# Inputs and outputs in the kernel's own shapes: q turned, k and v stacked, weights tiled before the launch

## The chip, the cores and the metric

One core of a Trainium2 chip. The metric is the device time of one execution in microseconds, the median of the runs. Engines: TensorE (PE: matmul; PEld: its weight load), VectorE (DVE), ScalarE (ACT), GpSimd (POOL), and SyncE (SP), whose queue issues nearly all DMAs. TensorE's clock has two levels, 1.2 and 2.4 GHz; the profile gives the granted share of the upper one.

## The reference

`q`, `k`, `v` are 8 batches x 8 heads x 576 tokens x 64, in float32; `w_in` (512 x 2048) and `w_out` (2048 x 512) are handed over in float64.

```python
kv  = einsum('bhsd,bhse->bhde', k, v)          # 64 x 64 per head
out = einsum('bhsd,bhde->bhse', q, kv)
x   = out / sqrt(mean(out**2, -1) + 1e-6) * g_norm   # per token and head
x   = x.transpose(0, 2, 1, 3).reshape(4608, 512)
h   = x @ w_in
y   = (h * cos(h)) @ w_out                     # 4608 x 512, float32
```

## The kernel before

**Chunks and stages.** The 4608 tokens are cut into 9 chunks of 512. A chunk lies across one or two of the 8 blocks (batches) of 576. In each chunk the features of x are four pairs of heads, p = 0 to 3, a tile of 128 features x 512 tokens each. Every large product runs in three parts, as a float32 number is split into a high and a low half that TensorE takes at full rate: high x high, low x high, high x low. Chunks 0 to 2 are plain: for each of the 16 tiles j of `w_in` and `w_out` a step computes h (12 products of 512 columns) and adds to four accumulators (12 more). The steps' order is in `segments` (line 315): chunk 0 with j 0 to 3, chunk 1 with j 0 to 7, chunk 0 with j 4 to 15, chunk 1 with j 8 to 15, chunk 2. Step 4 is so the first of chunk 1. Chunks 3 to 8 go in pairs with seven products in place of eight; of the last pair, 7 and 8, the second product is made so too, with its output turned (features x tokens).

**Front and steady state.** Blocks 0 and 1 and chunks 0 and 1 have a path of their own (`kv_front_part`, `x_front_part`) in full float32: k'v is accumulated over 9 or 6 slices of tokens, q arrives with tokens in partitions, is turned by TensorE in four transposes, copied by ScalarE or VectorE into a `two` tile, and multiplied; then come the norm (ScalarE square, VectorE reduce, GpSimd power, VectorE multiply), another turn by TensorE, and the split into xhi and xlo. For the later blocks `kv_part` makes k'v: 512 tokens of a head in four slices and a fifth slice with the leftover 64 tokens, padded with zeros to 128 rows in `k_over`, `v_over`. `x_part` turns q with VectorE (32x32 blocks; the DMA brings it in pieces of 32 values). Chunks 2 to 4 (`THREE`) then take three products, with k'v as blocks on a diagonal; chunks 5 to 8 take two, with high and low halves packed beside each other, into two PSUM banks whose halves ScalarE and VectorE add. `kv_turn_part` repacks k'v between the two forms.

**Weights.** `w_part` makes float32 out of the float64 words: ScalarE reads the high word, ScalarE or VectorE the low word, two operations of VectorE join them, then ScalarE rounds to the high half and VectorE subtracts. The split tiles are also stored to DRAM and reloaded by the later chunks (`wq`, `wod`, `wos`), partly as sums (`sums_part`, `sums_out_part`).

**What sets the order.** The program is written by a planner (`Order`, line 50): generators ask for an engine and a duration, and at each point the work item with the earliest start goes next, on a tie that with the smallest priority. A priority is a due time plus an entry of the table `haste` (line 343, `put_off`); `step_off` shifts gates by a quarter of the entry. Where two engines are offered (`copiers`, `adders`, the low word), the planner takes the one that it expects to end first. The order is fixed in the program (`Pinned`), for SP's DMAs too. Tokens (`t_two` with five, `t_slot`, `t_bank`) stand for buffers. SP keeps at most eight transfers under way: each issue waits for the landing of the eighth before it.

**The end.** The last products leave turned; `leave` and `finale` turn them back with VectorE in 32x32 blocks and store them in pieces of 32 values, four DMAs a tile.

Nearly all instructions carry line 253, the wrapper that pins the order, so the profile is read by tile names and shapes.

Of the kernel before, what the change touches and what calls it, by code (L numbers as in the profile page):

```python
# [9 lines left out]
F32 = mybir.dt.float32  # L10
# [8 lines left out]

P = 128  # L20
# [5 lines left out]


# [171 lines left out]
def tile_kernel(  # L199
# [3 lines left out]
    k: bass.AP,  # L203
    v: bass.AP,
    g_norm: bass.AP,
    moe_w_in: bass.AP,
    moe_w_out: bass.AP,
# [3 lines left out]
    B, H, S, D = q.shape  # L211
    NT, DM = out.shape
    DFF = moe_w_in.shape[1]
    NP = H // 2
    NJ = DFF // P
    CH = 512
    NCH = NT // CH
# [5 lines left out]
    assert ST == D  # L223
# [4 lines left out]
    SF = 2 * S // P  # L228
    SP = 96
    SQ = S // SP  # L230
# [76 lines left out]
    k_over = const.tile([P, H, D], F32, name="k_over")  # L307
    v_over = const.tile([P, H, D], F32, name="v_over")
    for t in (k_over, v_over):
        pool.memset(t, 0.0)  # L310
# [21 lines left out]
    THREE = (2, 3, 4)  # L332
    ASIDE = (3, 4)

    def due(i):
# [7 lines left out]
    haste = {  # L343
        ('acc', 0): -22.3, ('acc', 1): -60.4, ('acc', 10): -24.7, ('acc', 11): 82.8, ('acc', 12): -40.9,
        ('acc', 13): 546.1, ('acc', 14): 62.7, ('acc', 15): -8.6, ('acc', 16): 1346.9, ('acc', 17): 182.9,
        ('acc', 19): 223.9, ('acc', 2): 245.4, ('acc', 20): 41.4, ('acc', 21): 469.9, ('acc', 22): -280.7,
        ('acc', 23): 10.3, ('acc', 24): -146.3, ('acc', 25): 53.8, ('acc', 26): 1836.1, ('acc', 27): 138.4,
        ('acc', 28): -1.3, ('acc', 29): -8.2, ('acc', 3): 7.7, ('acc', 30): 74.1, ('acc', 31): -138.7,
        ('acc', 32): 0.1, ('acc', 33): -261.8, ('acc', 34): -11.5, ('acc', 35): 2337.3, ('acc', 36): -151.0,
        ('acc', 37): -973.0, ('acc', 38): 134.4, ('acc', 39): 5.1, ('acc', 4): 833.1, ('acc', 40): 39.8,  # L350
        ('acc', 41): 6.6, ('acc', 42): -789.5, ('acc', 43): 21.8, ('acc', 44): -19.0, ('acc', 45): 71.8,
        ('acc', 46): -3.6, ('acc', 47): -203.1, ('acc', 5): 233.3, ('acc', 6): 171.0, ('acc', 7): -97.9,
        ('acc', 8): 605.9, ('acc', 9): -64.2, ('act', 0): -4.7, ('act', 1): -343.2, ('act', 10): -435.4,
        ('act', 11): -15.0, ('act', 12): 49.5, ('act', 13): 1.5, ('act', 14): 142.2, ('act', 15): 354.9,
        ('act', 17): 152.2, ('act', 18): 110.4, ('act', 19): -139.7, ('act', 2): 0.9, ('act', 20): -58.3,
        ('act', 21): -47.2, ('act', 22): -435.2, ('act', 23): 1.8, ('act', 24): 43.9, ('act', 25): 7.6,
        ('act', 26): 47.9, ('act', 27): 4.6, ('act', 28): 50.6, ('act', 29): 236.4, ('act', 3): 37.6,
        ('act', 30): 4.8, ('act', 31): 55.4, ('act', 32): -148.1, ('act', 33): 146.1, ('act', 34): -1.6,
        ('act', 35): 10.6, ('act', 37): 48.3, ('act', 38): -3.0, ('act', 39): -35.2, ('act', 4): -93.7,
        ('act', 40): -126.6, ('act', 41): 254.3, ('act', 42): -133.3, ('act', 43): 71.5, ('act', 45): 112.7,  # L360
        ('act', 46): 148.3, ('act', 47): 530.0, ('act', 6): -5.1, ('act', 7): -6.8, ('act', 8): 26.3,
        ('act', 9): -250.2, ('combine by', 0, 0, 0): -12.5, ('combine by', 0, 0, 1): 479.5,
# [12 lines left out]
        ('cross', 0, 1): -12.2, ('cross', 1, 0): 327.2, ('cross', 1, 1): 659.3, ('cross', 2, 0): 132.8,  # L375
        ('cross', 2, 1): -59.2, ('fin', 0, 0): 199.4, ('fin', 0, 1): 34.5, ('fin', 0, 3): 782.3,
        ('fin', 0, 4): 21.1, ('fin', 0, 6): -37.3, ('fin', 0, 7): -143.6, ('fin', 1, 0): -26.5, ('fin', 1, 1): -3.5,
        ('fin', 1, 2): 126.4, ('fin', 1, 3): -24.4, ('fin', 1, 5): 171.4, ('fin', 1, 7): -2.8, ('fin', 2, 1): 15.2,
        ('fin', 2, 2): 2.6, ('fin', 2, 3): 437.1, ('fin', 2, 4): -402.0, ('fin', 2, 5): -194.2,
        ('fin', 2, 6): -186.8, ('fin', 2, 7): 227.9, ('fin', 3, 1): -283.5, ('fin', 3, 2): 1.6, ('fin', 3, 3): 27.7,  # L380
        ('fin', 3, 4): -31.5, ('fin', 3, 5): 196.1, ('fin', 3, 6): 214.6, ('fin', 3, 7): 166.8, ('fin', 4, 0): 53.6,
        ('fin', 4, 1): 16.5, ('fin', 4, 2): -114.1, ('fin', 4, 3): 203.6, ('fin', 4, 4): 39.6, ('fin', 4, 5): 134.7,
        ('fin', 4, 6): -188.8, ('fin', 4, 7): 10.3, ('fin', 5, 0): -127.7, ('fin', 5, 1): 146.9,
        ('fin', 5, 3): -81.5, ('fin', 5, 4): 98.9, ('fin', 5, 5): 100.8, ('fin', 5, 6): 25.0, ('fin', 5, 7): 109.9,
        ('fin', 6, 0): -147.6, ('fin', 6, 1): -13.5, ('fin', 6, 2): -21.2, ('fin', 6, 3): -25.8,
        ('fin', 6, 4): -193.3, ('fin', 6, 5): -30.4, ('fin', 6, 6): 438.9, ('fin', 6, 7): 408.9,
# [157 lines left out]
    def chunk_parts(c):  # L544
        parts, t = [], c * CH
        while t < (c + 1) * CH:
# [3 lines left out]
            t = e  # L550
        return parts

    def front_rows(c):

        if c == 0:
            return [(0, 0, P, 0), (0, 0, P, 1)]
# [1458 lines left out]
```

## Time and profile before

| | |
|---|---|
| runs | 822.45, 822.56, 823.3 us; median 822.56 |
| profiled execution, span | 823.5 us; no other time of it is given |
| TensorE busy | 808.5 us (98%), 4319 matmul instructions |
| VectorE, ScalarE, GpSimd busy | 658.0 (80%), 519.6 (63%), 315.7 us (38%) |
| DMA | 195.90 MB, 238 GB/s; 92080 of 183794 packets under 512 B |
| granted clock | 0.998 of full speed |

Busy times count each engine's instructions; an engine may be busy and yet wait for nothing that matters. In the trace a tile name stands for a buffer that serves several purposes: `wi` and `wo` hold weights, but in front also k, v, q and k'v; `m` and `sg` are the two halves of a `two` tile; `bank` and `acc` are PSUM. In a matmul row `128*64 128x64` means 128 rows and 64 columns of the array in use and a result of 128 x 64 places; a full float32 product is several instructions. Matmul records overlap, so what one costs is read from the distance of starts.

### The profile page before, as it was taken

What the parts mean: (1) busy time and instruction counts of PE and PEld (TensorE: products, weight loads), DVE (VectorE), ACT (ScalarE), POOL (GpSimd) and SP (SyncE); (2) the same over time, 40 slices, a digit from 0 to 9 for tenths busy, and PEclk for the clock granted to TensorE, in tenths of its full rate; (3) what the DMA queues carried; (4) which work ended last, traced back from release to release, by engine and by line L of the source; (5) the groups of instructions that cost most, each with busy time, mean ns of one, the idle gap of its engine ahead of it and who ended that gap; (6) DMA issues with size and microseconds to landing.
All of it is one profiled execution on the core that took longest, in us unless ns stands there. A gap on an engine that the chain in (4) does not pass through costs nothing.

```text
span 823.5 us, 12898 instructions
## 1 busy us (share of the span) xinstructions
PE 808.5 (98%) x4319; PEld 668.4 (81%) x4319; DVE 658.0 (80%) x1032; ACT 519.6 (63%) x1014; POOL 315.7 (38%) x212
## 2 busy tenths in 40 slices
PE   8889999999999999999999999999999999999997
PEld 7668888888888888887888888888888888888886
DVE  4989999568588897899997368889788888787862
ACT  5857897446545556787885646786586666675440
POOL 3234203136253352234567702224544402353450
PEclk9999999999999999999999999999999999999999
DMA  9997535667656858797797777897887788757763
GB/s 292 341 337 283 197 120 180 219 168 257 153 130 208 288 171 281 241 280 271 215 305 242 260 259 240 259 335 228 277 238 247 257 281 305 254 183 255 212 191 58
DMA packets 183794, 195.90 MB, mean 238 GB/s; under 512 B 92080, under 2 KB 145840, under 8 KB 183728
## 3 DMA queue, kind: packets, MB, share of 16 engines
q1 hardware_dynamic: 182672, 194.95, 75.4%
q8 instruction: 34, 0.56, 0.3%
q14 instruction: 32, 0.26, 0.1%
q10 hardware_dynamic: 1056, 0.13, 0.1%
HBM read 149.95 MB, written 45.09 MB: 237 GB/s over the span
## 4 chain that ended last, share of the span: by engine, by line
PE 91%; DMA 5%; DVE 2%; ACT 1%; SPq 0%; issue 0%; POOL 0%; ACTq 0%; POOLq 0%; DVEq 0%
PE bank L253 51%; PE acc L253 39%; DMA wo<-in_moe_w_out_dram 2%; DMA wi<-in_moe_w_in_dram 1%; DMA wi<-in_v_dram 1%; DMA wo<-wq 1%; DMA wi<-in_q_dram 1%; DVE sg L253 1%; SPq L253 0%; DVE r L253 0%; DVE glo L253 0%; ACT slot L253 0%; ACT sg L253 0%; POOL sg L253 0%; ACT wi L253 0%
## 5 line engine op out<-in xcount | busy, mean ns | idle before, releaser
L253 PE MATMUL bank<-wi,wo 128*128 128x512 f32 (+2 forms) x1284 | 287.7, 379 | 2.2 <-DMA wi<-in_v_dram 1.6
L253 PE MATMUL acc<-wo,ghi 128*128 128x512 f32 x896 | 277.1, 390 | 0.0
L253 PEld LDWEIGHTS bank<-wi,wo 128*128 128x128 f32 (+2 forms) x1284 | 227.0, 184 | 50.6 <-issue 2.4
L253 PEld LDWEIGHTS acc<-wo,ghi 128*128 128x128 f32 x896 | 167.1, 188 | 34.3
L253 PE MATMUL acc<-wo,glo 128*128 128x512 f32 x448 | 174.6, 390 | 0.0
L253 POOL TENSOR_TENSOR rinv<-ms,mhalf 128x16 f32<-128x16 f32 (+1 forms) x36 | 98.9, 2757 | 130.5 <-DVE ms L253 130.2
L253 PE MATMUL bank<-xhi,wi 128*128 128x512 f32 x320 | 99.6, 392 | 0.1
L253 PEld LDWEIGHTS acc<-wo,glo 128*128 128x128 f32 x448 | 84.1, 188 | 17.7
L253 DVE TENSOR_TENSOR wi<-bank,wi 128x512 f32<-128x512 f32 x72 | 49.2, 686 | 28.7 <-PE bank L253 23.8
L253 PEld LDWEIGHTS bank<-xhi,wi 128*128 128x128 f32 x320 | 59.5, 188 | 12.8 <-ACT wo L253 0.5
L253 ACT ACTIVATE ki<-wi 128x512 int32<-128x512 f32 x72 | 45.2, 628 | 28.6 <-DVE wi L253 24.7
L253 PE MATMUL bank<-xlo,wi 128*128 128x512 f32 x160 | 62.4, 390 | 0.0
L253 ACT COPY wi<-bank 128x512 f32<-128x512 f32 x72 | 42.0, 585 | 22.3 <-PE bank L253 21.2
L253 ACT ACTIVATE ki<-bank 128x512 int32<-128x512 f32 x72 | 42.7, 593 | 19.7 <-PE bank L253 15.2
L253 ACT ACTIVATE r<-r 128x512 f32<-128x512 f32 x60 | 37.8, 629 | 22.1 <-DVE r L253 20.9
L253 ACT CAST ghi<-r 128x512 fp32r<-128x512 f32 x57 | 35.3, 620 | 25.5 <-PE acc L253 24.6
L253 DVE TENSOR_TENSOR glo<-r,ghi 128x512 fp32r<-128x512 f32 x51 | 39.3, 773 | 13.8 <-ACT ghi L253 13.5
L253 ACT ACTIVATE wo<-wo 128x512 f32<-128x512 f32 x59 | 37.0, 629 | 15.7 <-DVE wo L253 15.0
L253 ACT CAST ghi<-wo 128x512 fp32r<-128x512 f32 x44 | 27.3, 619 | 23.7 <-PE acc L253 22.7
L253 DVE TENSOR_TENSOR r<-r,bank 128x512 f32<-128x512 f32 x50 | 33.9, 679 | 4.7 <-ACT r L253 3.8
L253 DVE SCALAR_TENSOR_TENSOR r<-bank,ki 128x512 f32<-128x512 f32 x51 | 34.7, 681 | 2.8 <-ACT ki L253 2.4
L253 POOL TENSOR_TENSOR glo<-wo,ghi 128x512 fp32r<-128x512 f32 x18 | 24.3, 1348 | 31.6 <-ACT ghi L253 30.3
(230 smaller groups left out, 1325.0 us busy)
## 6 DMA issues: line engine op xcount, KB each, us to landing
wo<-wq SPq DMA_DIRECT2D x84, 512.0 KB, 4.7
wo<-wod SPq DMA_DIRECT2D x64, 512.0 KB, 5.0
wi<-in_moe_w_in_dram SPq DMA_DIRECT2D x16, 512.0 KB, 10.1
wo<-in_moe_w_out_dram SPq DMA_DIRECT2D x16, 512.0 KB, 10.0
wod<-wo SPq DMA_DIRECT2D x16, 512.0 KB, 4.0
wo<-wos SPq DMA_DIRECT2D x16, 512.0 KB, 3.6
out_dram<-slot SPq DMA_DIRECT2D x28, 256.0 KB, 4.3
wq<-wi SPq DMA_DIRECT2D x24, 256.0 KB, 3.6
```

The source lines that it names most:

```text
L253: return lambda *a, **kw: tc.keep_in_program_order(f(*a, **kw))
```

## The change

`kernel()` now prepares the arrays: q transposed to features x tokens per chunk and pair; k and v stacked per block and pair into tiles of 128 partitions, of which each holds eight slices of 64 values and, behind them, the leftover tokens of head 0 in partitions 0 to 63 and of head 1 in 64 to 127; g_norm twice; weights tile by tile with 4 KB per partition. The kernel writes its output tile by tile, and `kernel()` transposes those of chunks 7 and 8 and joins them. Removed are the turns of q (TensorE in front, VectorE later) and of the last outputs, `k_over`, `v_over`, the packed two-product form with `kv_turn_part`. In front, k'v runs over the same five slices as later, kv_front has one block-diagonal tile per pair instead of two padded ones, and the x product of chunk 1 takes five pieces per pair instead of ten. `sums_out_part` gets a wait. The table of priorities is replaced as a whole (`HASTE`, not shown but for the entries of the first loads).

```diff
-def tile_kernel(ctx, tc, q, k, v, g_norm, moe_w_in, moe_w_out, out)
+def tile_kernel(ctx, tc, q, kv, g_norm, wi_words, wo_words, out)
...
+    ('load kv', 0, 0): -10.9, ('load kv', 0, 2): 102.7, ('load kv', 1, 0): -1.9, ('load kv', 1, 3): -1.6,
+    ('load q', 0, 2): -15.0, ('load q', 0, 3): -6.3, ('load q', 1, 1): -14.3, ('load q', 1, 3): 194.8,
...
     def kv_loads(b, p):
-            kv_tiles[b, p] = [two(slot, [P, 2, SI, D], F32, n) for n in range(2)], slot
-            for t, src in zip(kv_tiles[b, p][0], (k, v)):
-                sync.dma_start(
-                    out=t, in_=src[b, 2 * p:2 * p + 2, 0:SI * P, :].rearrange("h (p i) d -> p h i d", i=SI))
+            kv_tiles[b, p] = [two(slot, [P, KV], F32, n) for n in range(2)], slot
+            for n, t in enumerate(kv_tiles[b, p][0]):
+                sync.dma_start(out=t, in_=kv[b, p, n])
...
     def q_loads(c, p):
-            for b, s0, o0, n in chunk_parts(c):
-                for j in range(2):
-                    for f in range(2):
-                        ...
-                        sync.dma_start(out=qb[...], in_=q[...].rearrange("(tb t) d -> t tb d", t=32))
+            t = at.tile([P, CH], F32, name=f"qb{slot}", bufs=1)
+            sync.dma_start(out=t, in_=q[c, p])
...
+    def kv_products(ps, kt, vt):
+        def parts(i, j):
+            if i < SI:
+                cols = slice((SI * j + i) * D, (SI * j + i + 1) * D)
+                return kt[:, cols], vt[:, cols]
+            return kt[rows_of[j], KV - D:KV], vt[rows_of[j], KV - D:KV]
+        for i in range(SI + 1):
+            for j, r in enumerate(rows_of):
+                lhs, rhs = parts(i, j)
+                pe.matmul(out=ps[r, :], lhsT=lhs, rhs=rhs, start=(i == 0), stop=(i == SI))
...
     def x_front_part(c, p, prio):
         yield "wait", [q_in[c, p]]
-        pair = yield "take", t_two, prio
-        ...
-        for n in range(NTT):
-            pe.transpose(out=ps_t[:, n * P:(n + 1) * P], in_=qn[:, n, :], identity=ident)
-        e, end = yield "run", copiers(), prio
-        qT = two(pair, [P, CH], F32, 0)
-        copy(e, qT, ps_t[:, 0:CH])
...
+        qT = q_tiles.pop((c, p))
+        for b, _, o0, n in parts:
+            t = o0
+            while t < o0 + n:
+                e = min(t - t % P + P, o0 + n)
+                pe.matmul(
+                    out=ps[t % P:t % P + e - t, t - t % P:t - t % P + P], lhsT=qT[:, t:e],
+                    rhs=kv_front[b][:, p, :], start=True, stop=True)
+                t = e
...
     def x_part(c, p, prio):
-        dve.transpose(out=qT, in_=qb.rearrange("p a b -> p (a b)"))
-        if c in THREE:
-            yield from x_blocks(c, p, prio, parts, qT, slot)
-            return
-        ... (two products into two banks, halves joined)
+        qT, q_slot = q_tiles.pop((c, p))
         qhi, qlo = (two(slot, [P, CH], F32R, j) for j in range(2))
-        e, end = yield "run", copiers(), prio
-        copy(e, qhi, qT)
+        e, end = yield "run", [("ACT", act_us(), 0.0), ("DVE*", dve_us(), 0.3)], prio
+        copy(e.rstrip("*"), qhi, qT)
...
     def sums_out_part(m, prio):
+        yield "wait", [wo_kept[2 * m], wo_kept[2 * m + 1]]
         yield "take", t_sums, prio
...
         def finale(bank, v):
-            dve.transpose(out=o, in_=bank)
-            store(LAST, 1, v, o, slice(0, CH), [sync, act, sync, act])
+            act.copy(out=o[:, 0:half], in_=bank[:, 0:half])
+            act.dma_start(out=out[LAST, 2 + v, :, 0:half], in_=o[:, 0:half])
+            dve.tensor_copy(out=o[:, half:CH], in_=bank[:, half:CH])
+            sync.dma_start(out=out[LAST, 2 + v, :, half:CH], in_=o[:, half:CH])
...
 def kernel(**inputs):
+    arrays["q"] = q.transpose(1, 3, 0, 2).reshape(NP, P, NCH, CH).transpose(2, 0, 1, 3)
+    kv = _np.stack([x.reshape(B, NP, 2, S, D) for x in (k, v)], 2)
+    main = kv[:, :, :, :, :SI * P].reshape(B, NP, 2, 2, P, SI, D).transpose(0, 1, 2, 4, 3, 5, 6)
+    over = kv[:, :, :, :, SI * P:].reshape(B, NP, 2, P, D)
+    arrays["kv"] = _np.concatenate([main.reshape(B, NP, 2, P, 2 * SI * D), over], -1)
...
+    tiles = [x.reshape(CH, CH) for x in got]
+    return _np.concatenate([x.T if c in TURNED else x for c, x in enumerate(tiles)], 0)
```

## Rows read from the trace of the kernel before

**Rows 1.** Chain of waits from 60 us: start, duration, what.

```profile
64.84 9.55 PE bank L253 x42
...
136.95 16.32 PE bank L253 x72
```

**Rows 2.** Busy us (count) per engine by stretch; granted clock, DMA share, GB/s.

```profile
0.00:26.57 26.57, 21.54 (x316) 18.54 (x316) 14.85 (x32) 15.96 (x38) 11.35 (x17) 1.00 0.99 294
26.57:63.70 37.13, 32.63 (x232) 24.18 (x230) 33.07 (x57) 25.37 (x53) 11.62 (x7) 1.00 1.07 348
63.70:818.55 754.85, 754.28 (x3777) 625.68 (x3775) 609.31 (x944) 478.25 (x924) 292.78 (x189) 1.00 0.74 232
```

**Rows 3.** Chain of waits up to 70 us.

```profile
7.89 7.96 DMA wi<-in_v_dram
```

**Rows 4.** DMA issues up to 32.6 us: count, KB each, us to landing.

```profile
wi<-in_moe_w_in_dram SPq DMA_DIRECT2D x8, 512.0 KB, 9.6
wo<-in_moe_w_out_dram SPq DMA_DIRECT2D x5, 512.0 KB, 10.2
```

**Rows 5.** Timeline of VectorE: start, duration, what, idle time before it.

```profile
45.09 0.43 DVE L253 TENSOR_SCALAR m<-wo 128x512 int32<-128x512 uint32 x1 [2.56 <-DMA wo<-in_moe_w_out_dram]
```

**Rows 6.** Timeline of SP's issues.

```profile
39.44 5.34 SPq L253 DMA_DIRECT2D wo<-in_q_dram  x3
```

**Rows 7.** Groups of instructions up to 64 us: busy us, mean ns, idle before.

```profile
L253 ACT COPY m<-bank 128x512 f32<-128x512 f32 x8 | 4.5, 586 | 1.7 <-PE bank L253 1.7
...
L253 DVE TENSOR_SCALAR m<-wi 128x512 int32<-128x512 uint32 x4 | 1.7, 422 | 0.0
...
L253 DVE COPY wo<-bank 64x64 f32<-64x64 f32 x6 | 1.3, 224 | 6.8 <-ACT wo L253 5.1 <-PE bank L253 1.7
...
L253 DVE TENSOR_SCALAR m<-wo 128x512 int32<-128x512 uint32 x3 | 1.3, 424 | 2.6 <-DMA wo<-in_moe_w_out_dram 2.6
```

**Rows 8.** Timeline of TensorE around four q products, first and next piece.

```profile
169.42 0.34 PE L253 MATMUL bank<-m,kv_w 128*128 128x128 f32 x2
...
170.29 0.40 PE L253 MATMUL acc<-wo,ghi 128*128 128x512 f32 x1
...
215.20 0.37 PE L253 MATMUL bank<-m,kv_w 128*128 128x192 f32 x2
...
215.97 0.62 PE L253 MATMUL bank<-xhi,wi 128*128 128x512 f32 x2
...
365.58 0.41 PE L253 MATMUL bank<-m,kv_w 128*128 128x320 f32 x2
...
366.08 0.41 PE L253 MATMUL acc<-wo,ghi 128*128 128x512 f32 x1
...
411.68 0.41 PE L253 MATMUL bank<-m,kv_w 128*128 128x384 f32 x2
...
412.21 0.68 PE L253 MATMUL acc<-wo,ghi 128*128 128x512 f32 x2
```

**Rows 9.** Timeline of TensorE, begin of a k'v product.

```profile
161.04 0.39 PE L253 MATMUL acc<-wo,glo 128*128 128x512 f32 x1
161.36 0.69 PE L253 MATMUL bank<-sg,m 128*64 128x64 f32 x16
161.88 0.29 PE L253 MATMUL bank<-v_over,k_over 128*64 128x64 f32 x4
161.99 0.64 PE L253 MATMUL bank<-sg,m 128*64 128x64 f32 x16
```

**Rows 10.** Timeline of the end, all engines.

```profile
818.59 0.72 DVE L253 STREAM_TRANSPOSE slot<-bank 128x512 f32<-128x512 f32 x1 [4.72 <-PE bank L253]
...
819.34 0.93 ACTq L253 DMA_DIRECT2D out_dram<-slot  x2
```

**Rows 11.** Busy us by stretches of 20 us.

```profile
120.00:140.00 20.00, 20.00 (x90) 16.55 (x89) 20.00 (x32) 17.50 (x32) 3.04 (x3) 1.00 0.55 155
140.00:160.00 20.00, 20.00 (x90) 16.57 (x89) 12.32 (x18) 8.74 (x16) 6.18 (x5) 1.00 0.81 270
```

More of the change, by code (lines that the diff above doesn't have):

```diff
@@ L538, in put_off @@
+    haste = HASTE
     def put_off(*key):
@@ L608, in g_part @@
         yield "wait", [kv_in[0, 1]]
-        _, end = yield "run", [("ACT", 0.4)], -11.0
-        for r in (slice(D, 2 * D), slice(0, D)):
-            act.activation(out=gcol[r, :], in_=gcol[0:D, :], func=AF.Copy, scale=INV_2PI)
+        _, end = yield "run", [("ACT", 0.2)], -11.0
+        act.activation(out=gcol, in_=gcol, func=AF.Copy, scale=INV_2PI)
         sched.fire(g_both, end)
@@ L727, in kv_front_part @@
         bank = yield "take", t_bank, prio
-        _, end = yield "run", [("PE", 0.7 if b else 1.05)], prio, D if b else 0
+        _, end = yield "run", [("PE", 0.65)], prio, D
         ps = ps_tile(bank)
         kt, vt = kv_tiles.pop((b, p))
-        heads = [slice(j * D, (j + 1) * D) for j in range(2)]
-        n = SQ if b else SF
-        for i in range(n):
-            for j, r in enumerate(heads):
-                lhs, rhs = (t[0:SP, j, i, :] if b else t[r, i, :] for t in (kt, vt))
-                pe.matmul(out=ps[r, 0:D], lhsT=lhs, rhs=rhs, start=(i == 0), stop=(i == n - 1))
+        kv_products(ps[:, 0:D], kt, vt)
         sched.fire(kv_used[b, p], end)
@@ L740, in copies @@
         def copies(j):
-            e, end = yield "run", [("ACT", 0.41, 0.0), ("DVE", 0.45, 0.3)], prio
-            for r in heads:
-                copy(e, kv_front[b][r, 2 * p + j, r], ps[heads[j], 0:D])
+            e, end = yield "run", [("ACT", 0.2, 0.0), ("DVE", 0.22, 0.1)], prio
+            r = rows_of[j]
+            copy(e, kv_front[b][r, p, r], ps[r, 0:D])
             sched.fire(done[j], end)
@@ L832, in kv_split_part @@
         yield "wait", [kv_done[b, p] for p in range(NP)]
-        front = kv_front[b].rearrange("p (n j) d -> p n j d", j=2)
-        rows = [slice(j * D, (j + 1) * D) for j in range(2)]
-        end = yield from kv_parts(b, [front[r, :, j, r] for j, r in enumerate(rows)], prio)
+        end = yield from kv_parts(b, [kv_front[b][r, :, r] for r in rows_of], prio)
         for p in range(NP):
@@ L939, in x_part @@
         sched.fire(x_took[c, p], 0.0)
-        yield "take", t_qT
-        _, end = yield "run", [("DVE", dve_us())], prio
-        qT = at.tile([P, CH], F32, name="qT", bufs=1)
-        qb, q_slot = q_tiles.pop((c, p))
-        dve.transpose(out=qT, in_=qb.rearrange("p a b -> p (a b)"))
-        sched.give(t_q, end, q_slot)
-        rows = [slice(j * D, (j + 1) * D) for j in range(2)]
-        if c in THREE:
-            yield from x_blocks(c, p, prio, parts, qT, slot)
-            return
-        qs = [two(slot, [P, CH], F32R, j) for j in range(2)]
@@ L951, in x_part @@
-        for j, r in enumerate(rows):
-            yield "run", [("ACT", act_us())], prio
-            act.copy(out=qs[j][r], in_=qT[r])
-            e, end = yield "run", adders(CH, put_off("x by", c, p)), prio
-            adder(e).tensor_tensor(out=qs[j][rows[1 - j]], in0=qT[r], in1=qs[j][r].bitcast(F32), op=ALU.subtract)
-        sched.give(t_qT, end)
-        yield "wait", [(kv_turned if b in turned else kv_done)[b, p] for b, _, _, _ in parts]
-        yield "take", t_pair, prio
-        banks = []
@@ L960, in x_part @@
-        for j in range(2):
-            yield "take", t_psa, prio
-            banks.append((yield "take", t_bank, prio))
-        _, end = yield "run", [("PE", sum(2 * max(0.11, (n + 32) / 2400) for _, _, _, n in parts))], -1.0
-        both = [ps_tile(bank) for bank in banks]
-        for j in range(2):
-            for b, s0, o0, n in parts:
-                pe.matmul(
-                    out=both[j][:, o0:o0 + n], lhsT=kv_w[:, b % 2, 2 * p + j, :], rhs=qs[j][:, o0:o0 + n],
-                    start=True, stop=True)
@@ L970, in x_part @@
-        sched.fire(q_used[c, p], end)
-        sched.give(t_two, end, slot)
-        x, held = yield from x_place(c, prio)
-        for j, r in enumerate(rows):
-            ps = both[j]
-            yield "run", [("ACT", act_us())], prio
-            act.copy(out=x[r], in_=ps[rows[1 - j], 0:CH])
-            _, end = yield "run", [("DVE", dve_us())], prio
-            dve.tensor_tensor(out=x[r], in0=ps[r, 0:CH], in1=x[r], op=ALU.add)
-            give_ps(banks[j], end)
-        sched.give(t_pair, end)
@@ L1259, in out_part @@
         if complete:
-            sync.dma_start(out=rows(c, t), in_=o)
+            sync.dma_start(out=out[c, t], in_=o)
         else:
@@ L1851, in part_done @@
             elif v == 0:
[L1852 removed]
+                sched.spawn(leave(LAST, 1, 0, bank, 0.5), t)
             else:
```

436 lines of the change are left out of this document (154 added, 282 removed), and 177 rows, old and new, of tables (HASTE, haste).

## Prediction, before the result was known

> **What bounds the kernel now.** I read the chain of waits first: from 64.84 us on its long pieces are matmuls [rows 1]. Next the busy times by stretch [rows 2]: from 63.70 to 818.55 us TensorE has 0.57 us of idle time in 754.85 at the full granted clock, so in there only TensorE's own work counts, and what another engine saves is worth nothing while it stays ahead. Before 63.70 it is different: only the four first steps of chunk 0 have run, 4 x 24 products of 512 columns, 21.8 us at the 0.227 us that one takes in a full stretch (16.32 us for 72 [rows 1]). The rest of these 63.70 us is the front: loads, attention products of chunks 0 and 1, weight splitting. There VectorE is the busiest engine after TensorE (33.07 of 37.13 us [rows 2]) and DMA is full (share 0.99 and 1.07). After the last matmul stands a tail of 823.5 - 818.55 = 4.9 us. So the time is: when step 4 (the first of chunk 1) starts, at 64.84 [rows 1]; plus the TensorE work from there; plus the tail. I price the change in these three.
>
> **The start of step 4.** Four terms.
> (a) Block 0's loads. The last of them was issued at 7.89 and landed at 15.85 [rows 3]. Up to there came block 0 (8 x 288 KB of k and v, 4 x 256 KB of q: 3.41 MB) and one 0.52 MB tile of w_in, 3.93 MB in all. The new priorities (base times plus HASTE) put every load of block 0 ahead of w_in. At the stretch's 294 GB/s [rows 2] the 0.52 MB are 1.8 us. The x product of a pair then no longer waits for four TensorE transposes and a copy out of PSUM (0.59 us each [rows 7]). I take 3.0 us: 1.8, two such copies in a row, nothing for the transposes. Bounds: 1.8 and 5.
> (b) The wait for weights. VectorE stood 2.56 us until 45.09 for a tile of w_out [rows 5]. Until 32.6 us eight tiles of w_in had been issued but five of w_out [rows 4], and the second half of chunk 1's q (512 KB) was issued only from 39.44 us [rows 6]. Steps 0 to 3 need four of each. By the new priorities all of block 1 and these eight tiles come before the fifth pair: 3.41 + 3.41 + 8 x 0.524 = 11.0 MB, at 294 to 348 GB/s 32 to 37 us, against 45 and more now. The wait goes: 2.6 us. Next in line is VectorE itself, not another load. Bounds: 1 and 2.6.
> (c) VectorE's own work in front. Splitting a weight tile has one operation, the low word, that the planner gives to ScalarE or VectorE; VectorE did seven of these at 0.42 us. ScalarE now loses 8 copies of 0.586 us (4.5 us busy [rows 7]) and half of its 64x64 copies, so it can take them: 7 x 0.42 = 2.9 us; I take 2.4, as such operations overlap in part.
> (d) VectorE's 6 small copies of k'v (0.224 us) become 3: 0.7 us. Bounds of (c) and (d) together: 0 (they stay where they are) and 3.6.
> Together 3.0 + 2.6 + 2.4 + 0.7 = 8.7: step 4 starts at about 56. TensorE's own front work falls too (32 transposes; 36 or 24 instructions of k'v per pair become 20; 20 of the x product become 10), but it idled in front, so this is no further term.
>
> **TensorE's work after that.**
> (e) Chunks 5 to 8 pass from two products per part (low and high words packed side by side) to three, as chunks 2 to 4 have. Both forms stand in the trace, start to next start. 320+192 columns: two 0.50 (365.58 to 366.08), three 0.77 (215.20 to 215.97): +0.27. 384+128: 0.53 and 0.87: +0.34. Chunk 8 has 512 in one piece: one more product, +0.23. Chunk 7 has 448+64: a short piece costs more than its share of columns (the smaller piece 128 in place of 192 made 0.07 of difference), so I take 0.36, between 0.23 and 0.41. Times four pairs of heads: 4 x 1.20 = 4.8 us, slower [rows 8]. All of it on the path, since TensorE is full there. Bounds 4.3 and 5.0.
> (f) The leftover 64 tokens are stacked: heads 0 and 1 in the two halves of the partitions, so these products use 64 rows instead of 128 padded ones. Instruction counts stay (16 + 4 per pair, 24 pairs). What changes between 128*64 and 64*64 forms costs is not in the trace. Nearest row: the first 16 after a change of form took 0.52 us (161.36 to 161.88), the next 16 took 0.47 (161.99 to 162.46) [rows 9]. One such 0.05 per pair: 24 x 0.05 = 1.2 us. Bounds: 0, and 0.26 per pair, 6.2: both ways, each with the 0.09 by which the matmul before the change is longer (0.32 from 161.04 to 161.36, in place of 0.23).
> (g) The one gap of 0.57 us [rows 2], a wait for a weight reload, may go: DMA loses the q loads in 128-byte pieces. Or another one comes. I take -0.6, bounds -0.6 and +3.
> Free in this stretch, hidden by TensorE: on VectorE 28 turns of q, 8 of the last outputs and the joining of the halves of chunks 5 to 8; on SP 208 q loads become 28; kv_turn goes. The new wait in sums_out (for wo_kept) holds SP's loads of that part, behind it the weight reloads; by the new gates the earliest of these parts starts near step 32 and the copies that it waits for are sent near steps 14 and 16, so I price it at nothing; uncovered it is a chain of two transfers, some 10 us of SP's queue.
>
> **The tail.** (h) VectorE's 0.72 us turn, then two DMA issues on each of two queues (0.93 us on ACT) [rows 10] become half a copy on each of two engines and one issue each: some 0.4 and 0.46 us. Gain 0.3 + 0.5 = 0.8; the landing stays. Bounds 0.3 and 1.5.
>
> **Sum.** -8.7 + 4.8 + 1.2 - 0.6 - 0.8 = -4.1 us. The profiled execution's span is 823.5 us, 0.9 above the median of the runs, 822.56, with nothing visible around it; the difference goes onto the median: 818.5 us.
>
> **Rivals.**
> Head half as good again. Now the first product of chunk 0 comes at 26.57 (where the second stretch of [rows 2] begins), 10.7 us after block 0's last landing. Without turns of q, and with the `two` tiles that these held free for the splitting, it could come 4 us after a landing at 14, at 18, and TensorE could run from there without its 4.5 us of idle time (37.13 - 32.63): step 4 at 51.7, -13.1 in place of -8.7, and (f) free: 822.56 - 13.1 + 4.8 - 0.6 - 0.8 = 812.9. For it: idle time of all engines in front. Against: VectorE is busy 89% there.
> Half the gain in the head. The order of loads helps but VectorE's stream in front is as long as before; (a) and half of (b) stay, -4.3: 822.56 - 4.3 + 4.8 + 1.2 - 0.6 - 0.8 = 822.9, the same as before. For it: no VectorE operation of the splitting or of x's norm is removed.
> Changing the array's form is dear: (f) at its upper bound 6.2 in place of 1.2, 823.5. The Trainium skill says, in "TensorEngine Tiling", section "Key Properties", that a change of tiling mode drains TensorE; each pair would pay it twice. By that rule alone the new form of the leftover products would lose here. The trace agrees only in part: 0.05 us show in [rows 9], at one change, and no run here shows one between 128 and 64 rows.
> Slower: the head's gain is given back. Place: steps 8 to 23, which need twelve new weight pairs; VectorE had 0.00 us of idle time from 120 to 140 [rows 11] while it split them. If TensorE comes there 8.7 us earlier and VectorE doesn't, TensorE waits up to 8.7 us; then (e) and (f) remain: 822.56 + 4.8 + 1.2 - 0.6 - 0.8 = 827.2. It decides from the point where the last pair is due earlier than VectorE is through. Against: step 23 starts 19 steps of 24 x 0.227 = 5.44 us after 64.84, at 168; VectorE falls to 12.32 of 20 us from 140 on, so some 25 us of slack stand against 8.7.
>
> **Chances.** Forecast 0.62, larger head 0.17, half the head 0.08, dear form 0.05, given back 0.08. The time is 818.5. The range reaches from below the second case, 811.5, to 823.0; outside are the last two, 0.13 together, and the edges of the others. What a measurement can tell here is 0.2%, 1.6 us: faster is the first two cases, 0.79; same the third and fourth, 0.13; slower 0.08. The forecast's own range is 815 to 821.
>
> **What would show it.** Step 4 (chunk 1's first products after the first 96) at 53 to 59 us. First product of chunk 0 before 24. Low words of the splitting mostly on ScalarE in front, no wait of VectorE for w_out over 1 us. Six products of 0.77 and 0.87 in chunks 5 and 6. A pair of k'v in steady state at 0.58 now, then up to 0.65. From the last matmul to the end some 4.1 us. Wrong if step 4 starts after 62, or if TensorE idles more than 4 us after it.

## The result: 0.6% slower, and the profile after

The changed kernel takes 828.57 us (median; 827.26 to 828.98) against 822.5 us of the kernel before beside it: 1.0062 times the time, 95% interval 1.0047 to 1.0078. A second series gave 828.36 us, 1.0067 (1.0053 to 1.0080). The forecast was 818.5 us, with a range up to 823.0. Slower was given a chance of 0.08.

The page of the changed kernel, busy times and DMA packets. TensorE is busy for 813.3 us instead of 808.5; all other engines lost work, and the packets halved.

```profile
PE 813.3 (99%) x4195; PEld 672.0 (81%) x4195; DVE 621.8 (75%) x973; ACT 481.8 (58%) x937; POOL 270.7 (33%) x177
...
DMA packets 90365, 195.84 MB, mean 237 GB/s; under 512 B 8768, under 2 KB 37696, under 8 KB 90304
```

Where the time lies is seen best by cutting each trace at two events: the first product of 512 columns, and the 121st (five steps' worth; counted in the trace). Busy times of the changed kernel by these stretches, up to the last product; columns as in [rows 2].

```profile
0.00:22.69 22.69, 14.90 (x179) 12.82 (x180) 12.02 (x25) 11.10 (x24) 10.09 (x15) 0.97 0.94 351
22.69:60.95 38.26, 38.26 (x238) 30.35 (x237) 35.38 (x62) 26.74 (x50) 10.99 (x7) 0.97 1.03 415
60.95:821.79 760.84, 760.13 (x3781) 628.84 (x3779) 573.96 (x887) 443.56 (x863) 249.58 (x155) 1.00 0.68 226
```

The same of the third trace of the kernel before (below), which is nearest to its median:

```profile
0.00:25.15 25.15, 21.10 (x315) 18.22 (x316) 14.73 (x32) 15.83 (x38) 11.34 (x17) 1.00 0.98 316
25.15:65.80 40.65, 37.69 (x256) 28.39 (x253) 37.77 (x62) 29.29 (x60) 15.39 (x11) 1.00 1.07 366
65.80:815.54 749.74, 749.14 (x3753) 621.50 (x3751) 605.27 (x939) 474.04 (x917) 288.11 (x184) 1.00 0.74 230
```

The reader sees three things. The first two stretches got shorter (22.69 + 38.26 against 25.15 + 40.65). The last got 11.1 us longer. And in the middle stretch TensorE, idle for 2.96 us before, now has no idle time at all, though its granted clock is 0.97: it has become the bound of the head.

In the kernel before, the 80 products of a later block's k'v take 2.48 us, from 161.36 us [rows 9] to the next product:

```profile
163.84 0.73 PE L253 MATMUL acc<-wo,ghi 128*128 128x512 f32 x2
```

The same of one block in the changed kernel, timeline of TensorE:

```profile
449.83 3.58 PE L396 MATMUL bank<-sg,m 128*64 128x64 f32 x80
453.33 0.73 PE L396 MATMUL acc<-wo,ghi 128*128 128x512 f32 x2
```

From start to next start 3.50 us. The row groups both forms under the first one's name; with forms kept apart, each pair is 16 products of 128 rows and 4 of 64. That it is the change between them that costs is shown by experiments 1, 2 and 8.

An x product of chunk 5 (answers to [rows 8], third pair of rows), three products of either piece: 325.40 to 326.17, forecast 0.77.

```profile
325.40 0.47 PE L396 MATMUL bank<-m,kv_w 128*128 128x320 f32 x2
325.71 0.31 PE L396 MATMUL bank<-sg,kv_w 128*128 128x320 f32 x1
325.85 0.36 PE L396 MATMUL bank<-m,kv_w 128*128 128x192 f32 x2
326.05 0.28 PE L396 MATMUL bank<-sg,kv_w 128*128 128x192 f32 x1
326.17 1.11 PE L396 MATMUL bank<-wi,wo 128*128 128x512 f32 x4
```

The chain of waits of the changed kernel around the first product (start, duration, what). From 23.04 us on it holds nothing but PE up to 465 us:

```profile
19.07 2.02 POOL rinv L396
...
21.11 0.70 DVE r L396
...
21.95 1.09 PE acc L396 x4
23.04 10.11 PE bank L396 x81
```

TensorE's timeline shows the wait before it, and the windows of 2 us what followed (the third number from the end is the granted clock):

```profile
18.31 0.66 PE L396 MATMUL acc<-ident,r 128*128 128x128 f32 x4
21.95 1.09 PE L396 MATMUL acc<-ident,r 128*128 128x128 f32 x4 [2.98 <-DVE r L396]
```

```profile
20.00:22.00 2.00, 0.05 (x1) 0.08 (x2) 1.74 (x4) 1.41 (x3) 1.08 (x1) 0.84 1.03 410
22.00:24.00 2.00, 2.00 (x7) 1.81 (x8) 1.80 (x4) 0.92 (x2) 0.00 (x0) 0.50 1.05 409
24.00:26.00 2.00, 2.00 (x8) 1.59 (x8) 2.00 (x4) 1.41 (x3) 0.00 (x0) 0.81 1.05 421
```

So the first products run in part at 0.50 of the full clock, the 1.2 GHz level, right after an idle stretch that the kernel before does not have there. (One of the traces of the kernel before shows that level too, later and without such a stretch: experiment 5.)

The end (answers to [rows 10]):

```profile
821.83 0.37 ACT L396 COPY slot<-bank 128x256 f32<-128x256 f32 x1 [4.85 <-PE bank L396]
822.23 0.37 ACTq L396 DMA_DIRECT2D out_dram<-slot  x1
822.23 0.42 DVE L396 COPY slot<-bank 128x256 f32<-128x256 f32 x1 [10.59 <-ACT slot L396]
822.69 0.33 SPq L396 DMA_DIRECT2D out_dram<-slot  x1
```

The two halves do not run side by side: VectorE starts after ScalarE has ended.

### The profile page after: what moved, and what is told of

It is laid out like the page before. It is cut to its first block, busy times and chain, and to the rows that moved or that the text cites. A ratio compares the mean times of both kernels' runs of the same rounds, so it can differ in the third digit from the quotient of the medians.

```text
span 825.5 us, 12133 instructions
## 1 busy us (share of the span) xinstructions
PE 813.3 (99%) x4195; PEld 672.0 (81%) x4195; DVE 621.8 (75%) x973; ACT 481.8 (58%) x937; POOL 270.7 (33%) x177
## 2 busy tenths in 40 slices
DMA packets 90365, 195.84 MB, mean 237 GB/s; under 512 B 8768, under 2 KB 37696, under 8 KB 90304
## 4 chain that ended last, share of the span: by engine, by line
PE 94%; DVE 2%; issue 2%; POOL 1%; DMA 0%; ACT 0%; SPq 0%; POOLq 0%; DVEq 0%
PE bank L396 53%; PE acc L396 40%; POOL rinv L396 1%; DMA wo<-in_kv_dram 0%; DVE r L396 0%; DVE wo L396 0%; DVE wi L396 0%; DVE ms L396 0%; ACT slot L396 0%; DVE xlo L396 0%; DVE slot L396 0%; ACT xhi L396 0%; ACT swp L396 0%; ACT ki L396 0%; DVE part L396 0%
## 5 line engine op out<-in xcount | busy, mean ns | idle before, releaser
L396 PE MATMUL bank<-wi,wo 128*128 128x512 f32 (+1 forms) x1260 | 287.9, 383 | 0.7 <-DVE wi L396 0.5
L396 PEld LDWEIGHTS bank<-wi,wo 128*128 128x128 f32 (+1 forms) x1260 | 226.4, 185 | 48.6 <-DVE wi L396 0.9
L396 POOL TENSOR_TENSOR rinv<-ms,mhalf 128x16 f32<-128x16 f32 (+1 forms) x36 | 100.7, 2799 | 165.7 <-DVE ms L396 164.6
L396 DVE TENSOR_TENSOR glo<-r,ghi 128x512 fp32r<-128x512 f32 x53 | 37.6, 711 | 14.3 <-ACT ghi L396 13.7
L396 POOL TENSOR_TENSOR glo<-wo,ghi 128x512 fp32r<-128x512 f32 x15 | 19.9, 1325 | 84.9 <-ACT ghi L396 73.7
L396 DVE SCALAR_TENSOR_TENSOR wo<-wi,ki 128x512 f32<-128x512 f32 x43 | 34.9, 811 | 3.4 <-ACT ki L396 3.1
```

The lines of the kernel that those rows point to most:

```text
L396: return lambda *a, **kw: tc.keep_in_program_order(f(*a, **kw))
```

## The experiments

The gains and losses below are against the 828.4 to 828.6 us of the changed kernel, or, where it is said, against the kernel before; every series had the kernel before beside it.

**1. The leftover products over all 128 rows.** k as stacked; v gets two column groups, each with zeros in the other head's rows.

```diff
-            return kt[rows_of[j], KV - D:KV], vt[rows_of[j], KV - D:KV]
+            return kt[:, KV - D:KV], vt[:, KV + (j - 1) * D:KV + j * D]
...
+    own = _np.zeros((B, NP, 2, P, 2, D), over.dtype)
+    own[:, :, 0, :, 0] = over[:, :, 0]
+    own[:, :, 1, :D, 0] = over[:, :, 1, :D]
+    own[:, :, 1, D:, 1] = over[:, :, 1, D:]
```

> The leftover products run over all 128 rows again: k as stacked, v in two column groups of which each is zero in the other head's rows. So the array keeps its 128*64 form through all 20 products of a pair. Theory A (the change of form is what costs): 80 products of k'v of a block go back from 3.51 us to about 2.39 in steady state, six blocks give 6.7 us; in front 8 pairs at some 0.25 us, of which only those count for which TensorE is late, 0 to 2 us. The last matmul ends 6.7 to 8.7 us earlier, some 820 to 822 us in all. Theory B (the stacked tiles themselves are slow to read, or k'v only looks longer because records overlap): 80 products stay at 3.3 us or more, and the time stays within 1 us of 828.6.

Measured: 821.38 us, 7.2 less; 0.9984 (0.9973 to 0.9996) of the kernel before. A block's k'v, timeline of TensorE:

```profile
170.48 2.55 PE L397 MATMUL bank<-sg,m 128*64 128x64 f32 x80
172.97 0.73 PE L397 MATMUL acc<-wo,ghi 128*128 128x512 f32 x2
```

2.49 us again, with the same 80 instructions on the same stacked k. Theory A holds: this one edit turns the change from slower into slightly faster.

**2. The leftover products of a block together.**

```diff
-    def kv_products(ps, kt, vt):
+    def kv_products(ps, kt, vt, slices=range(SI + 1)):
...
-        for i in range(SI + 1):
+        for i in slices:
...
         for p in range(NP):
+            kv_products(ps[:, p, :], *kv_tiles[b, p][0], range(SI))
+        for p in range(NP):
             (kt, vt), slot = kv_tiles.pop((b, p))
-            kv_products(ps[:, p, :], kt, vt)
+            kv_products(ps[:, p, :], kt, vt, [SI])
```

> In steady state the leftover products of a block's four pairs come together after the other products: per block two changes of the array's form in place of eight. Theory A (each change costs, whatever it computes): three of four pairs of changes go, 3 x 0.29 us x 6 blocks = 5.3 us less, 823.3 us. Theory B (products of 64 rows are slow in themselves, 0.29 us per four of them): no gain, 828.6 us.

In this order the sums of four pairs in one PSUM bank are begun before the first is ended, and the fifth slice then does not add to the other four (k'v of the later blocks is not the reference's); the instructions are the same. The Trainium skill, "PSUM — Partial Sum Buffer", section "The four PSUM rules", says that beginning a second sum in the same bank and quadrant makes the first one's next product overwrite; no trace here shows that by itself.

Measured: 823.66 us, 4.7 to 4.9 less, for 5.3 forecast. Timeline of TensorE, one block:

```profile
449.94 2.70 PE L396 MATMUL bank<-sg,m 128*64 128x64 f32 x80
452.57 0.73 PE L396 MATMUL acc<-wo,ghi 128*128 128x512 f32 x2
```

2.63 us with one change inside the block, 3.50 with seven, 2.48 with none: (3.507 - 2.482) / 7 = 0.146 and (2.627 - 2.482) / 1 = 0.145 us per change between 128 and 64 rows, either way (durations from start to start, to the nanosecond; a kernel's six blocks agree within 0.001 us). The products of 64 rows cost nothing more in themselves, so theory B falls.

**3. Matmuls on zeros in the gap.**

```diff
+        turned_front.append(c)
+        if len(turned_front) == NP:
+            idle = ps_tile(t_bank.free[-1][2])
+            for _ in range(45):
+                pe.matmul(out=idle[:, 0:P], lhsT=zeros, rhs=zeros, start=True, stop=True)
         for a in range(NTT):
             ...
```

> 45 matmuls on zeros stand in TensorE's queue before the last turns of x in front, where TensorE stood idle for 2.98 us from 18.97 us on and the granted clock then fell to its lower level until 24.8 us. Theory A (the idle time is what lowered the clock): the granted clock stays at the upper level from 20 to 30 us; the profiled run gains about 1.7 us, the others, whose mean clock was lower (0.996 against 0.998), up to 3.3: median 825.5 to 827. Theory B (the clock falls for another reason, or VectorE is the late one there anyhow): no gain, or a loss of up to the length of the filling.

Measured: 826.74 us, 1.6 to 1.8 less; four of six runs have a mean clock of 1.000, none of the changed kernel's nine has. Timeline of TensorE, and the window in which the changed kernel shows 0.50:

```profile
20.35 2.67 PE L396 MATMUL bank<-zeros 128*128 128x128 bf16 x45
23.29 0.66 PE L396 MATMUL acc<-ident,r 128*128 128x128 f32 x4 [0.27 <-DVE r L396]
```

```profile
22.00:24.00 2.00, 1.73 (x24) 1.54 (x22) 1.74 (x4) 0.89 (x3) 0.51 (x1) 1.00 1.05 410
```

With the stretch filled the clock does not fall there, and that is worth some 1.7 us in the median. (This trace has a low stretch earlier, at 0.50 from 12 to 14 us, after a wait of 1.43 us for a load and well before the first product.)

**4. Chunks 5 to 8 without the third product.**

```diff
-            for i, (w, x) in enumerate(((hi, qhi), (lo, qhi), (hi, qlo))):
+            for i, (w, x) in enumerate(((hi, qhi), (lo, qhi), (hi, qlo))[:3 if c < 5 else 2]):
...
-                    start=(i == 0), stop=(i == 2))
+                    start=(i == 0), stop=(i == (2 if c < 5 else 1)))
```

> Chunks 5 to 8 leave out the third product of the attention output (high half of k'v with low half of q), so this part of the result lacks its last bits; all else is as in the changed kernel. If the third product is on the path at its full length, as TensorE is busy there: 4 x (0.26 + 0.29 + 0.31 + 0.23) = 4.4 us less, 824.2 us. If TensorE waits there for something else: 0 to 2 us.

Measured: 823.87 us, 4.5 to 4.7 less. The product of chunk 5, timeline of TensorE (the row holds all four instructions):

```profile
326.39 0.66 PE L396 MATMUL bank<-m,kv_w 128*128 128x320 f32 x4
326.89 1.34 PE L396 MATMUL bank<-wi,wo 128*128 128x512 f32 x5
```

0.50 against 0.77: the third product is on the path at its full length.

**5. The kernel before, traced twice more.** Its runs' times are 1.8 us above their spans, and so are the changed kernel's; the trace that the prediction read has a span of 823.5 us, so that execution took some 825.3, not 823.5.

> The kernel before once more, for a second trace. Its runs have spans of 819.8 to 823.5 us at times 1.8 us above them, most near 820.6, while the trace that the prediction read has a span of 823.5. Theory A (that trace was of a late execution, about 3 us late in the front): here the span is near 820.6, step 4 starts at 61 to 63 us instead of 64.84, and VectorE's wait for the tile of w_out is under 1 us instead of 2.56; then the head of the changed kernel gained some 5 to 6 us and not 8.5. Theory B (the traced execution was ordinary in front and lost its time later): step 4 starts at 64 to 65 us again.

> The kernel before a third time, for how much one trace differs from the next: by theory A step 4's start lies within 1.5 us of that of the second trace where the spans agree to 1 us, and later by as much as the span is longer.

| trace | span | first product | step 4 | 121st product | last product ends |
|---|---|---|---|---|---|
| before, first | 823.5 | 26.57 | 64.84 | 68.79 | 818.55 |
| before, second | 821.8 | 26.09 | 64.10 | 68.05 | 816.91 |
| before, third | 820.4 | 25.15 | 61.85 | 65.80 | 815.54 |
| after, first | 825.5 | 22.69 | | 60.95 | 821.79 |
| after, second | 827.2 | 23.47 | | 62.64 | 823.55 |

Step 4 in the table is the place at which the chain of waits of the kernel before comes to its first long piece of matmuls [rows 1]. The changed kernel has no such place, as its chain is one of matmuls from 23.04 us on, so the two kernels are compared at the 121st product.

VectorE's timeline, its wait for the same tile of w_out as in [rows 5], in the second and the third trace:

```profile
44.32 0.43 DVE L253 TENSOR_SCALAR m<-wo 128x512 int32<-128x512 uint32 x1 [0.91 <-DMA wo<-in_moe_w_out_dram]
```

```profile
42.08 0.43 DVE L253 TENSOR_SCALAR m<-wo 128x512 int32<-128x512 uint32 x1 [0.92 <-DMA wo<-in_moe_w_out_dram]
```

The 2.56 us were that one execution's. Theory A holds in the main; step 4 of the second trace, at 64.10, is later than the 61 to 63 expected, as its span is longer; the third starts step 4 2.25 us before the second at a span 1.4 shorter, and has a wait of 0.60 us later, at 694.91. Some 1.5 of the 2.25 us are TensorE's clock, which was low for 3.4 us in the second trace, although TensorE had waited no longer than 0.9 us at a time since 16 us; the third trace keeps the upper level there (busy time of TensorE between first and 121st product: 39.23 us in the second, 37.69 in the third). Windows of the second:

```profile
30.00:32.00 2.00, 1.96 (x5) 1.61 (x6) 2.00 (x4) 0.83 (x2) 0.00 (x0) 0.59 1.11 272
32.00:34.00 2.00, 2.00 (x8) 1.60 (x7) 1.19 (x3) 0.61 (x2) 0.00 (x0) 0.56 1.05 335
```

From the 121st product to the end of the span it is 753.8 to 754.7 us in all three, so an execution of before is long or short by its head. The median span, 820.9 (57 runs), puts the 121st product at some 66.5; the changed kernel's, 826.6 (9 runs), less the 764.5 to 764.6 of its two traces, at some 62.0. The head's gain is so about 4.5 us and not the 7.8 that the first two traces show.

**6. The changed kernel again.**

> The changed kernel once more, beside the next one and with more runs: 828.6 us again within 0.7, the granted clock at its lower level for some 3 to 7 us between 18 and 30 us, and 80 products of a later block's k'v at 3.5 us.

Measured: 828.36 us, as expected; the last row of the table. TensorE's wait of 2.98 us stands there too, at 19.74 us, and the mean clock is 0.995: the lower level lasts from 20.6 to 27.5 us, 6.8 us in place of the first trace's 3.4, and from the first to the 121st product it takes 39.17 us in place of 38.26. A block's 80 products take 3.51 us.

**7. Sixty more matmuls in the head.**

```diff
                 h = ps_tile(bank)[:, 0:CH]
+                if i == 2:
+                    for _ in range(60):
+                        pe.matmul(out=h[:, 0:P], lhsT=zeros, rhs=zeros, start=True, stop=True)
```

> The changed kernel with 60 matmuls on zeros (60 x 0.056 us = 3.3 us of TensorE's time, no other engine's) before the first product of step 2, at some 34 us. Theory A (from the first product of chunk 0 on TensorE is the bound of the head, so that the time saved on VectorE there could not count): the time rises by all of it, 3.3 us, to 831.7. Theory B (VectorE or the loads still set when step 4 starts, as the prediction had it): the filling lies beside their work, 0 to 1 us.

Measured: 831.71 us, 3.3 more than 828.4, as theory A had it. Timeline of TensorE:

```profile
40.69 3.51 PE L396 MATMUL bank<-zeros 128*128 128x128 bf16 x60
44.01 0.71 PE L396 MATMUL bank<-m,wi 128*128 128x512 f32 x2
```

3.32 us from start to start, and all of it comes out at the end. The trace agrees, though its execution was slower than the median: 42.63 us from the first to the 121st product, against 39.17 in the second trace of the changed kernel, where the clock was low about as long. From step 2 on the changed kernel's head is bound by TensorE, and time saved on VectorE there is no longer worth anything. Between the first product and step 2 no run tests it; there it rests on TensorE's having no idle time.

**8. The form alone, in the kernel before.**

```diff
-  (kt[:, j, i, :], vt[:, j, i, :]) if i < SI else (t[:, 2 * p + j, :] for t in (k_over, v_over)))
+  (kt[:, j, i, :], vt[:, j, i, :]) if i < SI else (t[0:D, 2 * p + j, :] for t in (k_over, v_over)))
```

> The kernel before with one edit: the leftover products of the later blocks use 64 rows (partitions 0 to 63, where the tokens lie) in place of the 128 padded with zeros. The same sums, the same instructions. Theory A (the change of the array's form costs 0.29 us per pair, wherever it stands): 24 x 0.29 = 7.0 us more, 829.6 us, and a block's 80 products take 3.5 us in place of 2.39. Theory B (the cost belongs to something else in the changed kernel, such as where the stacked tiles lie): the time stays within 1 us of 822.6.

Measured: 829.85 us against 823.49 beside it, 6.4 more; 1.0084 (1.0066 to 1.0101). Timeline of TensorE, begin of a block:

```profile
158.28 0.69 PE L253 MATMUL bank<-sg,m 128*64 128x64 f32 x16
158.89 0.33 PE L253 MATMUL bank<-v_over,k_over 64*64 64x64 f32 x4
159.16 0.69 PE L253 MATMUL bank<-sg,m 128*64 128x64 f32 x16
```

The first 16 take 0.61 us up to the next row and the four 0.27, where [rows 9] has 0.52 for a first 16, 0.11 for the four. A block's 80 products take 3.51 us, as in the changed kernel. Nothing of the rest of the change is in this kernel, so the cost is the form's alone.

**9. The three gains together.** Full rows, the filling, and a tile of its own for either half of a last output.

```diff
...
+            o2 = slot_tile((yield "take", t_slot, 0.0))
-            act.copy(out=o[:, 0:half], in_=bank[:, 0:half])
+            act.copy(out=o2[:, 0:half], in_=bank[:, 0:half])
...
```

> The changed kernel with three edits together: the leftover products over all 128 rows, the 45 matmuls on zeros in the gap, and a tile of its own for each half of a last output, so that VectorE's half of the copy doesn't wait for ScalarE's. If the single gains add up: 7.2 (rows) + 1.8 (clock) + 0.4 (the two copies of 0.37 and 0.42 us side by side) = 9.4 us less than 828.6: 819.2 us, 0.4% under the kernel before. If the gap's filling no longer fits the front, or the two gains are the same one in part: 820 to 821.5 us, no better than with the full rows alone.

Measured: 820.68 us, 0.9974 (0.9964 to 0.9984) of the kernel before: the best version here, faster than both. But it is only 0.7 us better than with the full rows alone, measured in another series, and the two intervals overlap. Two parts failed. The gap lies elsewhere in its trace (TensorE waits 2.23 us for a load of k and v until 18.71 us, ahead of the filling), and the zeros themselves then run at the low clock:

```profile
20.35 3.85 PE L397 MATMUL bank<-zeros 128*128 128x128 bf16 x45
```

```profile
20.00:22.00 2.00, 2.00 (x19) 1.94 (x18) 0.82 (x3) 1.44 (x4) 1.02 (x1) 0.50 1.03 417
```

Four of its twelve runs have a mean clock of 1.000 and spans of 817.8 to 817.9, three have 0.996 and 819.7 to 820.7. Where the front's gaps fall depends on when the loads land, so a filling in one place helps in part of the runs. And the two halves of the last copy stay one behind the other:

```profile
815.77 0.37 ACT L397 COPY slot<-bank 128x256 f32<-128x256 f32 x1 [4.85 <-PE bank L397]
...
816.18 0.42 DVE L397 COPY slot<-bank 128x256 f32<-128x256 f32 x1 [10.59 <-ACT slot L397]
```

It was not the shared output tile. Both read the same PSUM bank; the Trainium skill, "PSUM — Partial Sum Buffer", section "PSUM bank collisions raise a hardware error", says that two engines must not access one bank on the same partitions at once, and that the compiler puts such instructions in order. The trace agrees with that (VectorE starts 0.04 us after ScalarE's end); no run here took the bank apart.

**10. The packed two-product form put back as well,** for chunks 5 to 8, with the turn of k'v and the joining of halves as in the kernel before, and the filling in two places (20 and 25).

```diff
+        if c not in THREE:
+            ... (q split into two halves' tiles, two products into two banks, halves joined, as before)
...
+        if b in turned:
+            sched.spawn(kv_turn_part(b, due(i + 20) + put_off("kvt", b)))
...
+        if (b, p) == (0, NP - 1):
+            for _ in range(20):
+                pe.matmul(out=ps[:, 0:P], lhsT=zeros, rhs=zeros, start=True, stop=True)
```

> All that the runs so far point to, on top of the changed kernel: the leftover products over all 128 rows, the packed two-product form for chunks 5 to 8 as in the kernel before (with the turn of k'v and the joining of the two banks), a tile of its own for each half of a last output, and the zeros spread over both gaps (20 matmuls before the last pair's k'v in front, 25 before the last turn of x). From 820.7 us (the kernel with full rows, one filling and two tiles): minus 4.4 to 4.7 us of third products gives 816 us; with the clock at its upper level up to 1 us less. If ScalarE and VectorE, which get the joining back, become late, or the order of the work suits the packed form no longer: 818 us or more.

Measured: 850.92 us, a miss by 35. TensorE waits for VectorE in the very stretch where the packed form runs; timelines of TensorE and of VectorE:

```profile
453.96 0.80 PE L397 MATMUL acc<-wo,glo 128*128 128x512 f32 x1 [7.64 <-DVE glo L397]
```

```profile
450.59 1.65 DVE L397 TENSOR_TENSOR sg<-qb,sg 64x512 fp32r<-64x512 f32 x1
452.26 1.64 DVE L397 TENSOR_TENSOR glo<-wo,ghi 128x512 fp32r<-128x512 f32 x1
453.83 0.68 DVE L397 SCALAR_TENSOR_TENSOR xlo<-wi,ki 128x512 f32<-128x512 f32 x1
...
455.03 0.68 DVE L397 TENSOR_TENSOR glo<-wo,ghi 128x512 fp32r<-128x512 f32 x1
```

VectorE is busy for 76.6 of the 100 us from 400 to 500, so it isn't short of time; the `glo` that TensorE waits for stands in its queue behind a row of other operations. The two before 453.83 also take 1.65 and 1.64 us, where another `glo` takes 0.68 just after. GpSimd is in two operations of its own beside them, as its timeline shows, so some 1.9 of the 7.64 us may be the two engines in each other's way; no run takes them apart.

```profile
448.64 4.72 POOL L397 TENSOR_TENSOR wi<-xhi,wi 128x512 fp32r<-128x512 f32 x2 [3.44 <-ACT wi L397]
```

Over the whole trace TensorE is idle for 34 us, against 10 in that of experiment 9, and the mean clock is 0.986 against 0.997. The table of priorities was made for the three-product form. That this order is what fails here is argued from these rows and not shown by a run: which entries would have to change was not tried. What is shown is that the 4.4 us of experiment 4 are not to be had by putting the old form into the new order as it stands.

## Why the prediction was wrong, step by step

Forecast was -4.1 us; the medians show +5.9 (828.4 against 822.5). The parts, from the traces:

| | forecast | measured |
|---|---|---|
| head (a) to (d) | -8.7 | about -4.5 |
| (e) third products | +4.8 | +4.4 |
| (f) form of the leftover products | +1.2 | +6.15, and some in front |
| (g) gap | -0.6 | about +0.3 |
| (h) tail | -0.8 | -1.2 |

The measured ones add up to some +5.2; the last stretches of the traces leave some 0.6 us that I can't put down to a row, and the head's figure is worked out from medians.

**(f) failed first: mis-sized by 5.** "One such 0.05 per pair" took, once per pair, the smaller of the two figures that [rows 9] show at one change, between 128*128 and 128*64: 0.05 behind it, and 0.09 at the product before it, which only the upper bound counted. Together they are 0.14 us, nearly the price that the runs gave for the change between 128 and 64 rows: 0.146 us, at each change. So the trace had the size of it, though at another change. Of the eight changes in a block one, at the end, stands in the place of one that was there before: 7 x 0.146 = 1.025 us a block, six blocks: 6.15. The upper bound, 6.2, was the truth, in part by luck: its own figures, both ways, make 2 x (0.05 + 0.09) = 0.28 a pair and not 0.26, and the one change saved per block brings the measured 0.256. The rival "changing the array's form is dear" had this right in its mechanism; it came out too low, at 823.5, as it kept the head's gain. The Trainium skill's sentence in "TensorEngine Tiling (Array Packing)", section "Key Properties", that a change of tiling mode drains TensorE, bore on it, and experiments 1, 2 and 8 now agree with it, at 0.146 us a change. With ends as far apart as 0 and 6.2, taking the smaller figure once needed a reason, and the prediction gives none beyond "nearest row".

**The head failed second, by about 4.2,** in three places. Its term (a) held: the last pair of block 0's k'v starts at 13.61 and 14.39 us, in the traces of before at 14.85 to 15.98.
- (b) took 2.56 us from one row of one execution. The ordinary wait is 0.9 [experiment 5]. That the profiled execution had its own time "with nothing visible around it" was wrong: 1.8 us lie around the span in every run, and so that execution was 2.8 us later than the median, in the very head that I was pricing.
- "TensorE's own front work falls too, but it idled in front, so this is no further term" was the wrong way round. TensorE's idle time between first and 121st product was a ceiling: 2.96 us in the third trace of before, 4.50 in the first. (b), (c) and (d) were to save 5.7 there. TensorE now runs through without a gap, and what VectorE saves beyond that is lost [experiment 7]. The reading of [rows 2] was off as well: in its second stretch VectorE, at 33.07 us, is ahead of TensorE's 32.63 and not behind it. (c) came out smaller, too: VectorE still does three or four low words in front, so 1.3 to 1.7 us went for the 2.4 forecast; (d) held. Three of block 1's four pairs of k'v stand after the first product and pay for the form there, 0.58 us together (1.75 us for two and 0.88 for one, in place of 1.32 and 0.73 in experiment 1).
- The clock. First products came 3.0 us earlier than before in the median of the traces (26.09 to 23.08), as (a) said, and "before 24" held. But TensorE has some 180 instructions up to there in place of 316, with the turns of q gone. It had nothing left to do while the last pair's norm ran on GpSimd and VectorE, stood for 2.98 us, and its clock fell to the lower level: about 1.7 us given back [experiment 3]. Work taken from an engine that seems not to matter can leave it idle, and here that cost it its clock.

**(e) held:** 0.26, 0.29, 0.31 and 0.23 us per product of chunks 5 to 8 for 0.27, 0.34, 0.36 and 0.23, so 4.4 for 4.8 [experiment 4].

**(g)** was no fixed gap of the kernel before: 0.57 us in the first trace, none in the second, 0.60 elsewhere in the third. The changed kernel has 0.22 and 0.47, both waits for VectorE. So nothing was there to be gained.

**(h) held roughly in size, not in its way:** 4.90 to 3.69 us, 1.2 for 0.8. Up to the end of the last issue 0.5 us are gained (from 1.72 to 1.23 us after the last product), all by the fewer issues (0.33 us for one on SyncE, 0.93 for two on ScalarE before), as the half copies don't overlap. The other 0.7 us lie behind it, from the end of the last issue to the end of the span (3.18 to 2.46 us): the landing, which the prediction left as it was, got shorter.

**Of the signs named,** the low words came as forecast (seven of ten or eleven on ScalarE up to 62 us, three of ten before), and so did the wait for w_out (gone). A pair of k'v took 0.88 us for "up to 0.65". The 97th product, which was to come at 53 to 59 us, did so, at 55.38 and 57.07. But the kernel before has it at 59.33 to 62.35, and 64.84 is a later place, so this sign says little.

**Right were also** that nothing saved on VectorE, ScalarE and SP after the head counts, and that the new wait in `sums_out` costs nothing: no idle time over 0.5 us stands after the head. The rival "slower: the head's gain is given back" came to nearly the measured time, 827.2, by a mechanism that did not happen: TensorE never waited for VectorE in steps 8 to 23.

## What to carry to other kernels

Where one engine is the bound at 99%, count on it every change of the array's form, not only instructions and columns: padding to the same form was 7.2 us cheaper here than computing on fewer rows. Before pricing a head or a tail, take a second trace and see which waits repeat, and set as a ceiling on any gain from another engine the idle time that the next bound has in that stretch. An order made for one form of a product may not suit another: experiment 10 lost 30 us where 4.4 were to be gained.

## What the runs showed of the hardware

- A change between products of 128 and of 64 rows of the array costs TensorE 0.146 us, the same in both directions; the 64-row products are no slower in themselves (experiments 1, 2 and 8). A change from 128 to 64 columns at 128 rows costs about as much, 0.14 us [rows 9].
- Which waits lower TensorE's clock was not settled: it stayed at the upper level through the 2.32 us of the first trace of before, fell around a wait of 2.23 us in experiment 9 and of 2.98 in the changed kernel, and fell in the second trace of before with no wait over 0.9 us in the 14 us ahead of it. The lower level lasted 3.4 us in the changed kernel's first trace and 6.8 in its second; 3.4 us of it cost some 1.5 to 1.7 us where TensorE is the bound (experiments 3 and 5), and executions differ by that.
- With few packets under 512 B left (8768 for 92080) the DMA moved 404 to 415 GB/s between first and 121st product where it had moved 353 to 366, at about the same busy share (1.03 against 1.07). The order of the loads changed too, so no run shows the sizes alone as the cause. The time did not follow, as TensorE became the bound.
